# Chunked attention in transposed form on block-diagonal operands, placed between the matmuls of a feed-forward layer

## The chip, the cores and the metric

The kernel runs on one core of a Trainium2 chip. The metric is the time of one execution on the device in microseconds (us), the median over several runs. One execution of each kernel is also recorded by the hardware profiler; times inside a kernel are read from that record.

The engines: PE is TensorE (matmuls; PEld is its weight load), DVE is VectorE, ACT is ScalarE, POOL is GpSimd, SP is the sync engine, which here only issues DMAs.

## The reference

Attention inside chunks of 64 tokens, for 8 batches, 8 heads, 576 tokens and head dimension 64; its output, 4608 tokens of 512 numbers, goes through a feed-forward layer of width 2048 with exact gelu. The output is f32.

```python
scores = scale * np.matmul(q_c, k_c.transpose(0, 1, 2, 4, 3))      # 64 x 64 per chunk
scores = scores - np.max(scores, axis=-1, keepdims=True)
attn = np.exp(scores)
attn = attn / (np.sum(attn, axis=-1, keepdims=True) + 1e-09)
out = np.matmul(attn, v_c)
...                                     # heads side by side: x is (4608, 512)
h = x @ w_in                            # (512, 2048)
g = 0.5 * h * (1.0 + erf(h * inv_sqrt2))
return (g @ w_out).astype(np.float32)   # (2048, 512)
```

## The kernel before

Attention runs first, for all 64 pairs of batch and head; the feed-forward layer follows. Matmuls take bf16. Every small product goes to its own PSUM tile and is copied out by VectorE or ScalarE.

```python
    a_ps = ctx...tile_pool(name="a_ps", bufs=2, space=bass.MemoryType.PSUM)   # two buffers per tag
    ...
    for idx in range(B * H):
            for pi in range(NPAIR):              # transposes of q and k, 2 chunks at a time
                nc.tensor.transpose(tpq[0:CH*n_here, :], qb[:, c0:c0+n_here, :], identity_bf[:])
                nc.vector.tensor_copy(qT[0:CH*n_here, pi, :], tpq[0:CH*n_here, :])
                ...                              # the same for k, with nc.scalar.copy
            for c in range(NC):                  # NC = 9 chunks
                nc.tensor.matmul(sc_ps[:], qT[pp:pp+CH, pi, :], kT[pp:pp+CH, pi, :], tile_position=(pp, 0))
                ...                              # copy to sc_all, VectorE and ScalarE in turn
            nc.scalar.activation(ex[:], sc_all[:], mybir.ActivationFunctionType.Exp, scale=scale)
            ...                                  # row sums, reciprocal, product: attn_bf
            for c in range(NC):
                nc.tensor.transpose(atp[:], attn_bf[:, c, :], identity_bf[:])
                ...                              # copy to attn_T
            for c in range(NC):
                nc.tensor.matmul(o_ps[:], vb[:, c, :], attn_T[:, c, :])
                ...                              # copy to x_sbuf; odd heads by way of tmp and a DMA
    ...
    for mi in range(n_m_tiles):                  # 9 tiles of 512 tokens
        for nf in range(FF_sub):                 # 16
            for ks in range(K_sub):              # 4
                nc.tensor.matmul(h_ps[:], w_in_sbuf[:, ks, nf*P:(nf+1)*P],
                    x_sbuf[:, ks, mi*M_TILE:(mi+1)*M_TILE], start=(ks == 0), stop=(ks == K_sub - 1))
            nc.scalar.activation(h_sb[:, nf, :], h_ps[:], mybir.ActivationFunctionType.Gelu)
        for ms in range(n_m_subs):               # 4
            for nf in range(FF_sub):
                nc.tensor.matmul(y_ps[:], h_sb[:, nf, ms*P:(ms+1)*P], w_out_sbuf[:, nf, :],
                    start=(nf == 0), stop=(nf == FF_sub - 1))
            nc.vector.tensor_copy(y_sb[:], y_ps[:])
            nc.sync.dma_start(out_v[mi*M_TILE + ms*P : mi*M_TILE + (ms+1)*P, :], y_sb[:])
```

## Time and profile before

| | before |
|---|---|
| time, median | 665.89 us |
| span of the profiled execution | 664.4 us |
| attention, to the first feed-forward matmul | 410.1 us |
| feed-forward, its 1152 matmuls of 512 columns | 250.4 us |

The page of the kernel before. Part 1 gives busy time, share of the span and number of instructions of each engine; part 2 cuts the span into 40 slices and gives busy tenths in each.

```profile
span 664.4 us, 11364 instructions
...
PE 549.4 (83%) x3520; PEld 308.9 (46%) x3520; DVE 308.7 (46%) x1444; ACT 315.5 (47%) x1362; POOL 142.3 (21%) x200
...
PE   5468877777777777777777776999999999999997
...
DVE  4367777777777777677677773011010110101101
ACT  4346555565555555655555564432514325143250
```

PE is at 7 or 8 tenths up to slice 25 and at 9 from there on. That average hides two different stages. The table of stretches shows them apart (busy time and, in brackets, instructions that began, in 10 us of each stage):

```profile
core 0: us, PE busy (x) PEld busy (x) DVE busy (x) ACT busy (x) POOL busy (x), PEclk, DMA share, GB/s
300.00:310.00 10.00, 7.68 (x62) 5.03 (x61) 7.42 (x38) 5.55 (x32) 4.37 (x6) 1.00 0.70 48
450.00:460.00 10.00, 10.00 (x48) 4.53 (x47) 0.69 (x1) 2.89 (x5) 0.00 (x0) 1.00 0.07 26
```

In the second stretch PE is busy all the time with 217 ns a matmul (250.4 us / 1152), and everything else waits for it. (The clock of 1.00 in the first row can't be trusted: the trace's first record of the clock is at 413.4 us, and up to 413.0 us the feed-forward matmuls still start 0.427 us apart, half the later rate. The attention stage most likely ran at half clock.) In the first, no engine is full, and 62 small matmuls share 10 us. The chain of waits inside that stretch (start, length, what) says why:

```profile
301.70 0.27 PE atp L136 x2
301.99 0.21 ACT attn_T L138
302.21 0.04 issue
302.25 0.21 PE atp L136
302.50 0.21 ACT attn_T L138
```

Matmul, copy, matmul, copy: each link takes 0.2 us or a little more because the next matmul of the kind waits until one of two PSUM buffers has been copied out. Attention is bound by the latency of many small links, 6.4 us for each of 64 heads, and not by the throughput of an engine. This is read from the chain.

### The profile page before, as it was taken

The numbers are of one execution on the slowest core, as the hardware profiler recorded it, in microseconds if no ns is written. First come the engines' busy times: TensorE is split into PE (matmuls) and PEld (weight loads), VectorE is DVE, ScalarE is ACT, GpSimd is POOL, SyncE is SP. The second block draws the span as 40 slices with busy tenths as digits, with TensorE's granted clock in tenths as the row PEclk, the third lists the DMA queues.
The fourth block names the chain that finished last, engine by engine and source line by source line (L and its number), as shares of the span: only waits on it lengthen the run. The fifth ranks groups of instructions, "written<-read, shape, count | busy, mean of one in ns | idle before, by whom it ended". The sixth has DMA issues, their size and how long they took to land.

```text
span 664.4 us, 11364 instructions
## 1 busy us (share of the span) xinstructions
PE 549.4 (83%) x3520; PEld 308.9 (46%) x3520; DVE 308.7 (46%) x1444; ACT 315.5 (47%) x1362; POOL 142.3 (21%) x200
## 2 busy tenths in 40 slices
PE   5468877777777777777777776999999999999997
PEld 3244545454544554545454543444444444444443
DVE  4367777777777777677677773011010110101101
ACT  4346555565555555655555564432514325143250
POOL 9153333333332343333333100000000000000000
PEclk9999999999999999999999999999999999999999
DMA  9996566466656665665666200010010100101001
GB/s 86 207 117 46 42 46 46 34 48 47 44 40 45 43 47 40 47 47 39 43 48 42 20 8 8 16 48 32 33 65 16 48 32 33 64 16 48 35 30 63
DMA packets 144541, 30.90 MB, mean 47 GB/s; under 512 B 137312, under 2 KB 139360, under 8 KB 144480
## 3 DMA queue, kind: packets, MB, share of 16 engines
q0 software_dynamic: 116256, 18.36, 37.2%
q1 hardware_dynamic: 28224, 11.82, 6.5%
q8 instruction: 27, 0.44, 0.3%
q14 instruction: 34, 0.28, 0.1%
HBM read 36.70 MB, written 9.44 MB: 69 GB/s over the span
## 4 chain that ended last, share of the span: by engine, by line
PE 69%; ACT 12%; DMA 7%; DVE 6%; issue 5%; POOL 0%; ACTq 0%; DVEq 0%; POOLq 0%
PE h_ps L174 19%; PE y_ps L187 19%; PE atp L136 10%; DMA x_sbuf<-tmp 7%; PE o_ps L144 7%; ACT attn_T L138 6%; PE tpq L103 5%; PE tpk L106 5%; PE sc_ps L114 4%; DVE attn_bf L131 3%; ACT kT L107 3%; ACT x_sbuf L150 2%; DVE x_sbuf L148 2%; ACT ex L125 1%; ACT sc_all L122 0%
## 5 line engine op out<-in xcount | busy, mean ns | idle before, releaser
L181 ACT ACTIVATE h_sb<-h_ps 128x512 bf16<-128x512 f32 x144 | 85.9, 597 | 148.1 <-PE h_ps L174 148.1
L144 PE MATMUL o_ps<-attn_T,vb 64*64 64x64 bf16 x576 | 115.6, 231 | 31.4 <-ACT tmp L156 11.7
L136 PE MATMUL atp<-identity_bf,attn_bf 64*64 64x64 bf16 x576 | 100.4, 230 | 38.1 <-ACT attn_T L138 15.4
L195 DVE COPY y_sb<-y_ps 128x512 f32<-128x512 f32 x36 | 24.9, 692 | 226.3 <-PE y_ps L187 226.3
L174 PE MATMUL h_ps<-x_sbuf,w_in_sbuf 128*128 128x512 bf16 x576 | 127.4, 383 | 1.1 <-DVE tmp L154 1.1
L187 PE MATMUL y_ps<-w_out_sbuf,h_sb 128*128 128x512 bf16 x576 | 125.8, 379 | 0.0
L138 ACT COPY attn_T<-atp 64x64 bf16<-64x64 bf16 x320 | 65.3, 204 | 93.9 <-PE atp L136 71.7
L114 PE MATMUL sc_ps<-kT,qT 64*64 64x64 bf16 x576 | 100.3, 239 | 4.7 <-ACT sc_all L122 3.3
L103 PE MATMUL tpq<-identity_bf,qb 64*128 64x64 bf16 (+1 forms) x320 | 69.7, 218 | 30.5 <-ACT kT L107 22.4
L144 PEld LDWEIGHTS <-vb 64*64 64x64 bf16 x576 | 68.9, 135 | 45.0 <-issue 36.0
L174 PEld LDWEIGHTS <-w_in_sbuf 128*128 128x128 bf16 x576 | 56.6, 98 | 70.9 <-issue 2.2
L187 PEld LDWEIGHTS <-h_sb 128*128 128x128 bf16 x576 | 56.4, 98 | 67.9
L136 PEld LDWEIGHTS <-attn_bf 64*64 64x64 bf16 x576 | 63.4, 137 | 52.0 <-DVE attn_bf L131 28.0
L107 ACT COPY kT<-tpk 128x64 bf16<-128x64 bf16 (+1 forms) x320 | 66.3, 207 | 43.1 <-PE tpk L106 31.4
L72 POOL DMA_DIRECT2D kb<-in_k_dram x64 | 47.4, 740 | 173.5 <-PE tpk L106 99.8
L120 DVE COPY sc_all<-sc_ps 64x64 f32<-64x64 f32 x320 | 65.5, 211 | 24.0 <-PE sc_ps L114 21.3
L106 PE MATMUL tpk<-identity_bf,kb 64*128 64x64 bf16 (+1 forms) x320 | 71.6, 224 | 5.3 <-DMA kb<-in_k_dram 0.8
L114 PEld LDWEIGHTS <-qT 64*64 64x64 bf16 x576 | 54.4, 130 | 38.0 <-issue 30.9
L104 DVE COPY qT<-tpq 128x64 bf16<-128x64 bf16 (+1 forms) x320 | 55.2, 173 | 19.8 <-PE tpk L106 8.4
L71 POOL DMA_DIRECT2D qb<-in_q_dram x64 | 47.7, 746 | 44.4 <-PE o_ps L144 23.9
L140 DVE COPY attn_T<-atp 64x64 bf16<-64x64 bf16 x256 | 45.8, 179 | 23.8 <-PE atp L136 10.9
L122 ACT COPY sc_all<-sc_ps 64x64 f32<-64x64 f32 x256 | 52.7, 206 | 6.7 <-PE sc_ps L114 5.6
(21 smaller groups left out, 394.4 us busy)
## 6 DMA issues: line engine op xcount, KB each, us to landing
out_dram<-y_sb SPq DMA_DIRECT2D x36, 256.0 KB, 2.0
qb<-in_q_dram POOLq DMA_DIRECT2D x64, 72.0 KB, 2.8
kb<-in_k_dram POOLq DMA_DIRECT2D x64, 72.0 KB, 2.7
vb<-in_v_dram POOLq DMA_DIRECT2D x64, 72.0 KB, 2.8
x_sbuf<-tmp SPq DMA_DIRECT2D x288, 8.0 KB, 1.9
w_in_sbuf<-in_moe_w_in_dram POOLq DMA_DIRECT2D x1, 2048.0 KB, 14.4
w_out_sbuf<-in_moe_w_out_dram POOLq DMA_DIRECT2D x1, 2048.0 KB, 24.4
```

What stands on the lines that cost most here:

```text
L103: nc.tensor.transpose(tpq[0:CH*n_here, :], qb[:, c0:c0+n_here, :], identity_bf[:])
L104: nc.vector.tensor_copy(qT[0:CH*n_here, pi, :], tpq[0:CH*n_here, :])
L106: nc.tensor.transpose(tpk[0:CH*n_here, :], kb[:, c0:c0+n_here, :], identity_bf[:])
L107: nc.scalar.copy(kT[0:CH*n_here, pi, :], tpk[0:CH*n_here, :])
L114: nc.tensor.matmul(sc_ps[:], qT[pp:pp+CH, pi, :], kT[pp:pp+CH, pi, :], tile_position=(pp, 0),)
L120: nc.vector.tensor_copy(sc_all[:, c, :], sc_ps[:])
L136: nc.tensor.transpose(atp[:], attn_bf[:, c, :], identity_bf[:])
L138: nc.scalar.copy(attn_T[:, c, :], atp[:])
L144: nc.tensor.matmul(o_ps[:], vb[:, c, :], attn_T[:, c, :])
L174: nc.tensor.matmul(h_ps[:], w_in_sbuf[:, ks, nf*P:(nf+1)*P], x_sbuf[:, ks, mi*M_TILE:(mi+1)*M_TILE], start=(ks == 0), stop=(ks == K_sub - 1),)
L181: nc.scalar.activation(h_sb[:, nf, :], h_ps[:], mybir.ActivationFunctionType.Gelu)
L187: nc.tensor.matmul(y_ps[:], h_sb[:, nf, ms*P:(ms+1)*P], w_out_sbuf[:, nf, :], start=(nf == 0), stop=(nf == FF_sub - 1),)
```

## The change

The intent: cut the number of instructions of attention, and hide what is left of it behind the dense stream of the feed-forward layer.

- **Form.** Two heads are handled at once. Their keys, and their values, are laid out as blocks on the diagonal of 128x128 operands whose other blocks are zero. Scores come out transposed (keys on the partitions), so that exp of them can go straight into the value matmul: no transpose of the attention, no copy of the scores. Sums come from one matmul with a block-diagonal matrix of ones. The maximum is not subtracted, in either kernel.
- **Unit.** A unit is two heads times 512 tokens. There are 9 tiles of 512 tokens and 4 units in each. A unit has three parts: T (8 transposes, 3 copies on VectorE), S (8 score matmuls, an exp on ScalarE), B (the sum matmul, 8 value matmuls, 4 instructions on VectorE that divide and write x).
- **Placement.** The order is fixed by hand. T of tile t+1 stands between the first matmuls of tile t; S and B of tile t+1 stand between the second matmuls of tile t-1.
- **Loads.** q and k come in f32 as rows of 1 KB on the sync queue and are cast on GpSimd (tile 0: on VectorE and ScalarE). v comes by casting DMAs on the GpSimd queue into the zeroed diagonals.

The core of the diff, cut:

```diff
-    for idx in range(B * H):
-        ...
+    def att_T(t, g):
+        tp = ps_tp.tile([P, 2, J, P], bf16, tag="tp", name="tp")
+        for w, nm in enumerate(("q", "k")):
+            for j in range(J):                                          # J = 4
+                nc.tensor.transpose(tp[:, w, j, :], st[nm][:, g, j]..., ident[:])
+        nc.vector.tensor_copy(qT[:].rearrange("p i j c -> p j i c"), tp[:, 0]...)
+        for r in range(2):
+            sl = slice(CH * r, CH * (r + 1))
+            nc.vector.tensor_copy(
+                k_bd[sl, :, sl].rearrange("p i (c j) -> p j i c", j=J),
+                tp[sl, 1].rearrange("p j (i c) -> p j i c", i=CT))
+    def att_S(t, g):
+        for i in range(CT):                                             # 8 chunks
+            nc.tensor.matmul(s_ps[:, i, :], st["k_bd", g][:, i, :], st["qT", g][:, i], ...)
+        nc.scalar.activation(pT[:], s_ps[:], Act.Exp, scale=scale)
+    def att_B(t, g):
+        nc.tensor.matmul(sum_ps[:], ones_bd[:], pT[:], start=True, stop=True)
+        for i in range(CT):
+            nc.tensor.matmul(av_ps[:, i, :], st["v"][:, i, g, :], pT[:, i, :], ...)
+        nc.vector.transpose(t1[:], sum_ps[:]...)
+        nc.vector.reciprocal(r1[:], t1[:, :, 0])
+        nc.vector.transpose(rc[:], r1[:].to_broadcast([P, NB, 32]))
+        nc.vector.tensor_tensor(
+            x[:, g, :].rearrange("p (i c j) -> p i j c", i=CT, j=J),
+            av_ps[:]..., rc[:]..., op=mybir.AluOpType.mult)
+    with tc.manual_schedule():
+        new_tile(0)                     # loads of q, k, v of tile 0
+        ...                             # 4 DMAs of w_in
+        new_tile(1)
+        ...                             # 2 DMAs of w_out
+        new_tile(2)
+        T, S_, Bs = att_units(0)
+        for u in T + S_ + Bs:
+            u()
+        T, S_, Bs = att_units(1)        # issues the casts of tile 1 on GpSimd
+        run_phase(mm1_slot, 0, FF, {4: [T[0]], 5: [T[1]], 6: [T[2]], 7: [T[3]],
+                                    9: [S_[0]], 10: [S_[1]], 11: [S_[2], Bs[0]], 12: [S_[3]],
+                                    13: [Bs[1]], 14: [Bs[2]], 15: [Bs[3]]})
+        for t in range(1, NT):
+            ...                         # att_units(t + 1), new_tile(t + 2)
+            run_phase(mm1_slot, t, FF, {1: [T[0]], 5: [T[1]], 9: [T[2]], 13: [T[3]]} if nxt else {})
+            run_phase(mm2_slot, t - 1, 16,
+                      {1: [S_[0]], 3: [S_[1]], 5: [S_[2], Bs[0]], 7: [S_[3], Bs[1]],
+                       9: [Bs[2]], 11: [Bs[3]]} if nxt else {})
+        run_phase(mm2_slot, NT - 1, 16, {})
```

A slot is 4 matmuls of 512 columns, 0.86 us; a phase is 16 slots.

## The prediction

> **What bounds the kernel now.** Two stages follow one another. In the timeline the first feed-forward matmul (line 174) starts at 410.09 us and the last of line 187 ends at about 660.5; one VectorE copy (0.69 us) and a store end the span of 664.4 us. In the second stage PE is saturated: the table of stretches has it busy 240.0 of 240 us, and 1152 matmuls in 250.4 us are 217 ns each. The Trainium skill ("TensorE: Matmul & The Clock Gate", Back-to-back issue gap) gives N/2.4 + 2.5 ns, 216 at N=512; the trace agrees.
>
> The first 410 us are attention, 6.4 us a head, with no engine saturated. The chain of waits alternates matmul (0.21 us) and eviction (0.20 us) through two PSUM buffers per tile kind; costs are per instruction, over a thousand small ones each on PE, ACT and DVE.
>
> **What the change does.** (1) A unit is two heads by 512 tokens, 36 in all: 8 transposes, 8 score matmuls, one 512-wide sum matmul, 8 value matmuls. The transposes of the attention, the score copies and the 288 stores into x's upper half go. (2) Units of tile t+1 stand between matmuls of tiles t and t-1, so their DVE and ACT work hides under the 217 ns stream. (3) q and k come as 1 KB f32 rows on the sync queue and are cast on GpSimd; v comes by casting DMA into zeroed block diagonals.
>
> **Costs (estimates from the trace's durations).** DVE per unit: three evictions of 0.6 us, two 512-wide block transposes, a reciprocal (0.20), a product (0.74): 4.2 us, 150 in all, plus 25 for y: hidden. ACT: gelu 86 us, 36 exps of 0.6, some 25 table loads of 1.28: hidden except in the first phase. GpSimd per tile: 16 DMA issues of up to 0.74 and 8 casts of 0.8, against 35 us: hidden. PE per unit: 24 small matmuls at 0.08 to 0.10 us (a 128-column weight load lasts 98 ns) plus 0.22: 2.3 us, wholly on the critical path.
>
> **Sum.**
> - Prologue: 43 us. 18 zeroing memsets on DVE stand before the first casts (20 us), then casts, 4 units of evictions (7) and 4 chains of 2.6, with nothing to hide under.
> - First phase, tile 0: 13.8 + 4 x 2.3 + 10 of stalls (exps among gelus switch tables about 8 times, and tile 1's x is wanted at once): 33 us.
> - Sixteen phases of 13.8: 221; 28 units x 2.3: 64; stalls 5: 290 us.
> - Last 16 slots 13.8, copy and store 4: 18 us.
>
> Total **384 us**, range 358 to 425. Chances: faster by over 2% 0.98, within 2% 0.01, slower 0.01.
>
> **What would show it right or wrong.** PE is dense after 43 us; feed-forward matmuls stay 216 ns apart. The wait table has PE's main waits in the prologue and around tile 0's phase, little elsewhere. The chain of waits is over 80% PE. The prologue is wrong if the first h matmul starts before 34 or after 52 us; the unit cost is wrong if a tile's two phases take other than 27.6 + 9 us.
>
> **What would make it wrong.** GpSimd too slow (46 DMA issues stand ahead of tile 1's casts; or casts over 2 us); strided evictions much slower than 0.6 us; the last unit's product arriving late for the next phase, every tile; small matmuls over 0.12 us; start-up loads (over 12 MB asked for at once) holding back tile 0's q and k or the first weights.

## The result, and the profile after

The changed kernel takes 375.31 us (median of 4 runs, 374.62 to 376.38), against 665.66 us in the same rounds: a ratio of 0.5635, with a 95% interval of 0.562 to 0.565.

The page after, the lines that answer to those of before, with GpSimd and the granted clock added:

```profile
span 374.2 us, 5238 instructions
...
PE 305.2 (82%) x2052; PEld 154.5 (41%) x2052; DVE 239.6 (64%) x313; ACT 140.2 (37%) x208; POOL 125.2 (33%) x204
...
PE   0353500766899999999999999999999999999995
...
DVE  7989100696775975887598589759867965920221
ACT  2130200189564066236505622551563165254000
POOL 7321855989700007703920780270130000000000
PEclk9999955598999999999999999999999999999999
```

PE is dense from slice 12 on. But there is a hole in slices 6 and 7, from 43.7 us on, and the granted clock falls to one half there (slices 6 to 8). PE's waits (who waited for whom, total, times, longest):

```profile
PE tp L148 <- POOL q_nat L115: 22.6, 1, 22.6
PE tp L148 <- DVE q_nat L111: 12.8, 1, 12.8
PE av_ps L180 <- DVE x L190: 5.8, 7, 0.8
...
PE h_ps L212 <- DVE x L190: 4.3, 3, 2.4
```

One wait of 22.6 us for the casts of tile 1 on GpSimd is larger than all others. Once past the start, a tile looks like this in the timeline of PE (start, length, instruction, idle before it):

```profile
130.10 0.39 PE L148 MATMUL tp<-ident,q_nat 128*128 128x128 bf16 x4
130.33 0.39 PE L148 MATMUL tp<-ident,k_nat 128*128 128x128 bf16 x4
130.55 3.63 PE L212 MATMUL h_ps<-x,w_in_sb 128*128 128x512 bf16 x16
...
145.71 0.40 PE L167 MATMUL s_ps<-qT,k_bd 128*128 128x64 bf16 x8
145.95 1.89 PE L224 MATMUL y_ps<-w_out_sb,h 128*128 128x512 bf16 x8
...
149.87 0.38 PE L177 MATMUL sum_ps<-pT,ones_bd 128*128 128x512 bf16 x1
150.08 0.40 PE L180 MATMUL av_ps<-pT,v_bd 128*128 128x64 bf16 x8
150.32 1.89 PE L224 MATMUL y_ps<-w_out_sb,h 128*128 128x512 bf16 x8
...
153.48 0.41 PE L180 MATMUL av_ps<-pT,v_bd 128*128 128x64 bf16 x8 [0.82 <-DVE x L190]
```

The length of such a row includes the latency of the last matmul; the cost to the stream is the distance between starts. Eight transposes cost 130.55 - 130.10 = 0.45 us, eight score matmuls 0.24, the sum 0.21 and eight value matmuls 0.24: 1.14 us a unit. The only idle time on PE in the tile is 0.82 us, in the last line shown: the value matmuls of the second unit want a PSUM buffer that VectorE's product for the first unit still reads.

The sum of the prediction against the trace (the first matmul of tile 1 is worked out as 94.07 + 4 x 0.216 = 94.9 us, the start of the last 16 slots as 342.37 + 64 x 0.216 = 356.2 us, from rows that merge several phases):

| stretch | predicted | measured |
|---|---|---|
| prologue, to the unbroken feed-forward stream | 43 | 38.8 |
| first phase, tile 0, with the units of tile 1 | 33 | 56.1 |
| 16 phases with 28 units | 290 | 261.3 |
| last 16 slots, copy and store | 18 | 18.0 |
| sum | 384 | 374.2 |

The total was near, and two of its terms were off by some 25 us each, in opposite directions. The experiments ask about both, and about where the gain comes from.

**Theories.** (A) The hole comes from the order of GpSimd's instructions: the casts stand behind 46 DMA issues, some of which wait for the weights to land. Rival: the start is bound by DMA bandwidth, and the casts only show it. (B) A small matmul with its own weight load costs 0.03 us of the stream, and this is on the critical path. Rivals: 0.08 to 0.10 us, as predicted; or PE has slack. (C) The placement is worth as much as the form. Rival: the form alone does it. (D) VectorE's writes with a step are what makes its part long. (E) Table loads stall the first phase, as predicted; rival: they hide.

### The profile page after: what moved, and what is told of

It reads as the page before. It is cut to its first block, busy times and chain, and to the rows that moved or that the text cites. A ratio compares the mean times of both kernels' runs of the same rounds, so it can differ in the third digit from the quotient of the medians.

```text
span 374.2 us, 5238 instructions
## 1 busy us (share of the span) xinstructions
PE 305.2 (82%) x2052; PEld 154.5 (41%) x2052; DVE 239.6 (64%) x313; ACT 140.2 (37%) x208; POOL 125.2 (33%) x204
## 4 chain that ended last, share of the span: by engine, by line
PE 65%; DVE 14%; DMA 13%; POOL 4%; issue 2%; DVEq 0%; POOLq 0%
PE h_ps L212 30%; PE y_ps L224 28%; DMA w_in_sb<-in_moe_w_in_dram 7%; DVE x L190 4%; DMA w_out_sb<-in_moe_w_out_dram 4%; PE tp L148 4%; POOL v_bd L124 3%; DMA v_bd<-in_v_dram 3%; DVE rc L188 3%; DVE k_bd L157 3%; DVE t L184 3%; PE s_ps L167 1%; PE av_ps L180 1%; PE sum_ps L177 1%; DVE r L186 1%
## 5 line engine op out<-in xcount | busy, mean ns | idle before, releaser
L212 PE MATMUL h_ps<-x,w_in_sb 128*128 128x512 bf16 x576 | 138.1, 390 | 4.4 <-DVE x L190 4.3
L214 ACT ACTIVATE h<-h_ps 128x512 bf16<-128x512 f32 x144 | 85.5, 597 | 144.7 <-PE h_ps L212 144.5
L224 PE MATMUL y_ps<-w_out_sb,h 128*128 128x512 bf16 x576 | 132.5, 379 | 0.0
L124 POOL DMA_DIRECT2D v_bd<-in_v_dram x128 | 83.9, 713 | 29.4 <-DMA w_in_sb<-in_moe_w_in_dram 12.8
L157 DVE COPY k_bd<-tp 64x512 bf16<-64x512 bf16 x72 | 92.6, 1287 | 0.5
L212 PEld LDWEIGHTS <-w_in_sb 128*128 128x128 bf16 x576 | 55.7, 100 | 65.4 <-issue 9.3
L224 PEld LDWEIGHTS <-h 128*128 128x128 bf16 x576 | 53.5, 98 | 58.1
L115 POOL CAST q_nat<-q_f 128x512 bf16<-128x512 f32 x32 | 18.4, 637 | 106.8 <-PE h_ps L212 58.6
L190 DVE TENSOR_TENSOR x<-av_ps,rc 128x512 bf16<-128x512 f32 x36 | 46.5, 1292 | 4.1 <-DVE rc L188 0.5
L148 PE MATMUL tp<-ident,q_nat 128*128 128x128 bf16 x144 | 15.5, 236 | 39.7 <-POOL q_nat L115 22.6
L184 DVE STREAM_TRANSPOSE t<-sum_ps 128x512 f32<-128x512 f32 x36 | 25.7, 715 | 8.8 <-PE sum_ps L177 8.8
L188 DVE STREAM_TRANSPOSE rc<-r 128x512 f32<-128x512 f32 x36 | 25.6, 711 | 1.3
L115 POOL CAST k_nat<-k_f 128x512 bf16<-128x512 f32 x32 | 18.4, 628 | 8.5 <-DMA k_f<-in_k_dram 7.8
## 6 DMA issues: line engine op xcount, KB each, us to landing
k_f<-in_k_dram SPq DMA_DIRECT2D x2, 896.0 KB, 11.5
```

Source lines behind the costliest of these rows:

```text
L115: nc.gpsimd.tensor_copy(o[:, g], i_[:, g])
L124: nc.gpsimd.dma_start(v_bd[CH * r:CH * (r + 1), i0:i0 + n, g, CH * r:CH * (r + 1)], v[b, 2 * g + r, CH * cs:CH * (cs + n), :].rearrange("( ...
L148: nc.tensor.transpose(tp[:, w, j, :], st[nm][:, g, j].rearrange("p r d -> p (r d)"), ident[:])
L157: nc.vector.tensor_copy(k_bd[sl, :, sl].rearrange("p i (c j) -> p j i c", j=J), tp[sl, 1].rearrange("p j (i c) -> p j i c", i=CT))
L184: nc.vector.transpose(t1[:], sum_ps[:].rearrange("p (n e) -> p n e", e=32))
L188: nc.vector.transpose(rc[:], r1[:].to_broadcast([P, NB, 32]))
```

## The experiments

Twelve variants were run besides the changed kernel; all gave correct results.

| kernel | time, us | ratio to before |
|---|---|---|
| the changed kernel | 375.3 | 0.5635 |
| e1_cast_first | 359.6 | 0.5401 |
| e2_serial | 519.8 | 0.7806 |
| e3_slot8 | 381.0 | 0.5722 |
| e4_double | 381.7 | 0.5737 |
| e5_swap | 372.7 | 0.5600 |
| e6_group | 362.3 | 0.5438 |
| e7_three | 339.4 | 0.5098 |
| e8_four | 341.9 | 0.5127 |
| e9_best | 343.4 | 0.5153 |
| e10_wout_last | 366.5 | 0.5506 |
| e11_ungroup | 340.5 | 0.5115 |
| e12_prologue | 335.4 | 0.5038 |

### e2_serial: the form without the placement

```diff
+        for t in range(NT):
+            T, S_, Bs = att_units(t)
+            ...
+            for u in T + S_ + Bs:
+                u()
-        run_phase(mm1_slot, 0, FF, {4: [T[0]], 5: [T[1]], ...})
+        run_phase(mm1_slot, 0, FF, {})
         for t in range(1, NT):
-            run_phase(mm1_slot, t, FF, {1: [T[0]], ...} if nxt else {})
-            run_phase(mm2_slot, t - 1, 16, {1: [S_[0]], ...} if nxt else {})
+            run_phase(mm1_slot, t, FF, {})
+            run_phase(mm2_slot, t - 1, 16, {})
```

> All units of all nine tiles run before the first feed-forward matmul (x kept for nine tiles; some rotating buffers cut from 3 to 2 to make room); the transposed block-diagonal form is as in the changed kernel. Theory (the placement hides some 6 us of VectorE work per unit): attention becomes bound by VectorE at 6.0 us per unit, 36 x 6.0 = 215 us plus the start and the 23 us hole, and the feed-forward follows at 250 us: 490-520 us. Rival (the form alone does it, VectorE and PE of neighbouring units overlap by themselves and the placement adds little): under 430 us.

Measured: 519.8 us. The form alone takes 666.2 - 519.8 = 146 us off, the placement another 519.8 - 375.3 = 145 us: (C) holds, in this order: the parts of the form (pairs of heads on the diagonal, transposed scores, fewer and larger copies, other loads) were not run apart, nor was the placement without the form. Busy time in 100 us of the attention stage and in the feed-forward stage:

```profile
core 0: us, PE busy (x) PEld busy (x) DVE busy (x) ACT busy (x) POOL busy (x), PEclk, DMA share, GB/s
...
100.00:200.00 100.00, 40.18 (x407) 29.89 (x408) 92.09 (x115) 9.12 (x16) 63.73 (x103) 0.60 0.78 111
262.00:512.00 250.00, 250.00 (x1154) 112.94 (x1153) 29.49 (x43) 85.97 (x144) 0.00 (x0) 0.99 0.10 37
```

VectorE is busy 92 of 100 us there and PE 40. That is the work that the placement hides: while VectorE needs about 6 us a unit, the feed-forward stream runs beside it.

### e4_double: what does a small matmul cost?

```diff
-        for i in range(CT):
+        for i in list(range(CT)) * 2:
             nc.tensor.matmul(s_ps[:, i, :], st["k_bd", g][:, i, :], st["qT", g][:, i],
```

> Every score matmul is issued twice, the second writing the same values to the same place: 288 more matmuls of 64 columns, each with its weight load. Theory (PE's stream is the critical path and a small matmul with its own load costs what the trace's spacing shows, 0.029 us): 0.235 us per unit on 32 units in or near the stream: +7 to +9 us. By the prediction's 0.08 to 0.10 us each: +23 to +29 us. Rival (PE has slack in the steady part): +2 us or less.

Measured: 381.7 us, 6.4 us more, a little less than the 7 to 9 expected. In the steady state a tile takes 33.87 us (128.63 to 162.50) where the changed kernel takes 33.16 (129.24 to 162.40). The four units' added matmuls explain 4 x 0.24 = 0.94 us of that; 0.22 us came back, since the wait of 0.82 us at the second unit shrank to 0.60. So (B) holds: these matmuls are on the critical path, at 0.029 us each with their own weight load. The predicted 0.08 to 0.10 us would have given 23 us or more. The Trainium skill ("TensorE: Matmul & The Clock Gate", "Wait — 56ns, not 53.3ns?") gives about 25 ns as the least distance between two matmuls, however short; the 29 ns at 64 columns and 56 ns at 128 (0.45 us / 8) lie above that, and no run here tests the floor itself. What fits them is the formula N/2.4 + 2.5 that my prediction quoted for 512 columns only: it gives 29 and 56 ns. I should have used it instead of the 98 ns that a weight load lasts. The load lasts that long but overlaps its neighbours.

### e1_cast_first and e10_wout_last: the hole

```diff
         new_tile(1)
+        tiles[1]["cast"]()              # e1_cast_first: before w_out and the v loads of tile 2
         for c in range(2):
             ...                         # w_out
         new_tile(2)
         ...                             # att_units no longer issues the casts of tile 1
```

> The q and k casts of tile 1 on GpSimd are issued before the two DMAs of w_out and the v loads of tile 2; nothing else changes. Theory (GpSimd's order): PE's 22.6 us wait for q_nat comes from the 18 DMA issues that stand ahead of the casts and that wait in turn for w_in and w_out to land; q and k of tile 1 had landed long before. Then the wait falls to about 3 us, the cold matmuls after it go too, and the time falls by about 20 us, to 353-357. Rival (the start-up is bound by DMA bandwidth, the casts merely reveal it): the wait moves to w_out, v of tile 1 or other loads and the time falls by under 8 us, to 367 or more.

Measured: 359.6 us, 15.7 us less. What GpSimd did before the casts in the changed kernel, in its timeline:

```profile
27.75 0.56 POOL L124 DMA_DIRECT2D v_bd<-in_v_dram  x1 [3.22 <-DMA w_in_sb<-in_moe_w_in_dram]
31.97 0.75 POOL L124 DMA_DIRECT2D v_bd<-in_v_dram  x1 [3.66 <-DMA w_in_sb<-in_moe_w_in_dram]
36.25 0.55 POOL L124 DMA_DIRECT2D v_bd<-in_v_dram  x1 [3.52 <-DMA w_in_sb<-in_moe_w_in_dram]
39.23 6.02 POOL L124 DMA_DIRECT2D v_bd<-in_v_dram  x9 [2.43 <-DMA w_in_sb<-in_moe_w_in_dram]
45.16 1.87 POOL L247 DMA_DIRECT2D w_out_sb<-in_moe_w_out_dram  x2
46.91 3.96 POOL L124 DMA_DIRECT2D v_bd<-in_v_dram  x6
54.45 0.60 POOL L124 DMA_DIRECT2D v_bd<-in_v_dram  x1 [3.58 <-DMA w_out_sb<-in_moe_w_out_dram]
59.87 5.76 POOL L124 DMA_DIRECT2D v_bd<-in_v_dram  x9 [4.82 <-DMA w_out_sb<-in_moe_w_out_dram]
65.52 2.39 POOL L115 CAST q_nat<-q_f 128x512 bf16<-128x512 f32 x4
```

It issued the v loads of tile 1, w_out and the v loads of tile 2, four times waiting for a w_in DMA and twice for a w_out DMA to land, and reached the casts at 65.52 us. PE's transposes of tile 1 began at 66.31. With the casts earlier, PE's waits for them are:

```profile
PE tp L148 <- POOL q_nat L115: 4.3, 2, 3.4
...
PE tp L148 <- POOL k_nat L115: 3.4, 2, 1.8
```

The largest wait for a cast is 3.4 us instead of 22.6. (A) holds. The gain is 4 us less than expected, because the same thing now happens on a small scale to tile 2, whose casts still stand behind w_out: PE waits 0.97 and 1.81 us for them at 77 us, and the 16 matmuls after that take 5.30 instead of 3.62 us, since the clock had dropped.

Why did GpSimd wait for w_out to land at all? Count the DMAs on its queue (numbers 1 to 16 come before the lines above): 8 of v (tile 0), 4 of w_in, 16 of v (tile 1), 2 of w_out, 16 of v (tile 2). In the lines above, numbers 17 to 20 wait for w_in, which is numbers 9 to 12, and numbers 37 and 38 wait for w_out, numbers 29 and 30. Each waits for the one eight places before it. (The program's instruction list had the same as waits for semaphores.)

So in this program at most eight DMAs of that queue are under way, and a large one blocks what stands eight places behind it, casts included. The second experiment parts this from the plain time to issue:

```diff
-        for c in range(2):              # w_out, ahead of new_tile(2)
-            ...
         T, S_, Bs = att_units(1)        # the casts of tile 1
+        for c in range(2):              # e10_wout_last
+            ...
```

> The changed kernel with only the two DMAs of w_out moved behind tile 1's casts on GpSimd; the 16 v loads of tile 2 stay ahead of them. This parts the 22.6 us hole into the landing of w_out, which GpSimd waits for since each of its DMAs waits for the one eight before it (12 us with their own issue), and the plain issue of 16 loads (10.4 us). If so, PE's wait for q_nat falls to 10-14 us and the time to 363-367. If the issue time alone makes the hole: wait of 20 us or more. If the landing alone: under 5 us.

Measured: 366.5 us, and a longest wait of 13.4 us for the cast:

```profile
PE tp L148 <- POOL q_nat L115: 13.4, 1, 13.4
```

So some 9 us of the hole were w_out's issue and landing, 10 us the issue of the 16 v loads of tile 2, and the rest lay before that. In these runs bandwidth is part of the cause only through the waits for landing.

### e3_slot8: the wait of 0.82 us

```diff
-                      {... 5: [S_[2], Bs[0]], 7: [S_[3], Bs[1]], 9: [Bs[2]], 11: [Bs[3]]}
+                      {... 5: [S_[2], Bs[0]], 7: [S_[3]], 8: [Bs[1]], 10: [Bs[2]], 12: [Bs[3]]}
```

> The value units B1, B2 and B3 stand one slot later in the second feed-forward phase (slots 8, 10, 12 in place of 7, 9, 11); nothing else changes. Theory: PE waits 0.82 us in each of 7 tiles because B1's value matmuls want the PSUM buffer that B0's product on VectorE has not released; one slot of 0.86 us covers it. The waits for that product vanish in the steady tiles and the time falls by 5 to 6 us (1.5%). Rival: the wait only moves to the next unit or to the next tile's x (VectorE's chain of 2.95 us a unit sets the pace): change under 2 us.

Measured: 381.0 us, 5.7 us *more*. My theory fell. The wait at the second unit did vanish, but a larger one came:

```profile
PE tp L148 <- POOL q_nat L115: 24.8, 1, 24.8
PE h_ps L212 <- DVE x L190: 13.5, 10, 2.4
```

Ten waits of the feed-forward matmuls for x, 13.5 us in all, in place of three of 4.3. With the last unit one slot later, its product on VectorE ends after the next tile's first matmuls want x: about 1.3 us of waiting in each tile, against 0.82 saved. A tile went from 33.16 to 33.75 us (130.30 to 164.05). VectorE's chain of about 2.95 us a unit fixes when the last x is ready, and the placement had no room to give. The hole was also 2.2 us longer in this run (24.8 us).

### e5_swap: VectorE's strided writes

The same elements in another order: neighbours in the output come one after the other, and PSUM is read with a step.

```diff
-                k_bd[sl, :, sl].rearrange("p i (c j) -> p j i c", j=J),
-                tp[sl, 1].rearrange("p j (i c) -> p j i c", i=CT))
+                k_bd[sl, :, sl].rearrange("p i (c j) -> p i c j", j=J),
+                tp[sl, 1].rearrange("p j (i c) -> p i c j", i=CT))
 ...
-            x[:, g, :].rearrange("p (i c j) -> p i j c", i=CT, j=J),        # and av_ps, rc alike
+            x[:, g, :].rearrange("p (i c j) -> p i c j", i=CT, j=J),
```

> The changed kernel with only the order turned round in which VectorE walks the same elements in two instructions: the two k_bd evictions and the product into x now write neighbouring elements one after the other and read PSUM with a stride, in place of reading in runs and writing every fourth element. Theory (the write with a step of four 2-byte elements is what makes them 1.29 us): k_bd falls to 0.7 us or less, the product to 0.75-0.85 us, VectorE per unit from 6.0 to about 4.3 us; the 0.82 us waits in 7 tiles vanish (5.7 us), the prologue shortens by 4 x 1.7 = 6 to 7 us and the stretch of tile 1's units by some us; the hole at the casts grows by what the prologue wins, since GpSimd sets its end. Sum: 6 to 11 us less, 364-369. Rival (half of the partitions, or the PSUM read, is what is slow): durations stay within 10% or grow, and so does the time.

The groups of VectorE, first of the changed kernel, then of e5_swap (out<-in, shapes, count, busy us and mean ns of one, idle before):

```profile
L157 DVE COPY k_bd<-tp 64x512 bf16<-64x512 bf16 x72 | 92.6, 1287 | 0.5
L190 DVE TENSOR_TENSOR x<-av_ps,rc 128x512 bf16<-128x512 f32 x36 | 46.5, 1292 | 4.1 <-DVE rc L188 0.5
...
L150 DVE COPY qT<-tp 128x512 bf16<-128x512 bf16 x36 | 15.2, 423 | 51.6 <-PE tp L148 51.4
```

```profile
L157 DVE COPY k_bd<-tp 64x512 bf16<-64x512 bf16 x72 | 49.2, 684 | 0.5
L190 DVE TENSOR_TENSOR x<-av_ps,rc 128x512 bf16<-128x512 f32 x36 | 36.4, 1010 | 4.1 <-DVE rc L188 0.5
...
L150 DVE COPY qT<-tp 128x512 bf16<-128x512 bf16 x36 | 15.3, 424 | 89.0 <-PE tp L148 88.9
```

The k_bd copies went from 1287 to 684 ns and the product from 1292 to 1010 ns; the qT copy, which was not touched, stayed. So the order in which elements are walked was the cost, and not the half of the partitions: (D) holds for k_bd, and the product fell less than expected. The swap changed the read along with the write. But the qT copy reads PSUM in the same order as the k_bd copy of the changed kernel, writes runs of 16 neighbours and takes 423 ns, so the step of 4 in the write is what is left for the 1287. The Trainium skill ("SBUF — State Buffer", on cachelines of 16 bytes) says that steps of up to 8 bf16 elements run at full rate; here a step of 4 elements on the write side took nearly twice as long as the other order, so the measurement decides.

The time, 372.7 us, fell by 2.6 us only, less than the 6 to 11 expected. The wait of 0.82 us in each tile shrank to about 0.54 and did not vanish. And the prologue did get shorter, with the stream beginning at 33.25 us instead of 38.79, but PE then waited 29.9 us for the casts instead of 22.6. The hole swallowed the gain, and tile 1's transposes, which GpSimd's casts release, began at 67.99 us, later than the 66.31 of the changed kernel. This is the clearest lesson on the way: while one engine's order sets the end of a stretch, speeding up another engine there only lengthens the wait.

### e6_group, e7_three, e8_four, e11_ungroup: tables, and the causes together

e6_group is e1_cast_first with tile 1's exps in a row, so that ScalarE switches tables twice in the first phase in place of eight times:

```diff
-                                    9: [S_[0]], 10: [S_[1]], 11: [S_[2], Bs[0]], 12: [S_[3]],
+                                    9: [S_[0], S_[1], S_[2], S_[3]], 11: [Bs[0]],
```

> As e1_cast_first, with tile 1's four score units together in slot 9 of the first feed-forward phase, so that its four exps follow one another on ScalarE: the table loads in that phase go from about 8 to 2. Prediction's step (the table switches stall that phase by about 10 us): 6 to 10 us less than e1_cast_first (359.6). Rival (there it is VectorE's chain, 3 us per unit, that PE waits for, and ScalarE's loads hide behind it): within 2 us of e1_cast_first.

Measured: 362.3 us, 2.7 us *slower* than e1_cast_first. The six spared table loads of 1.28 us won nothing, and the fourth score unit now waits 2.5 us for a PSUM buffer. Nor does any wait of PE's in the changed kernel name ScalarE. So the predicted stall from table switches is not there: (E) falls. A switch cost 1.31 us between the end of a gelu (78.10 us in the changed kernel) and the start of the exp (79.41). The Trainium skill ("ScalarE: Activation LUTs", "What ACT_TABLE_LOAD costs") adds a drain of about 1.38 us to the load of 1.28; the trace shows none.

e7_three joins the three, with the casts of tiles 1 and 2 ahead of their v loads:

```diff
-        new_tile(1)
+        tiles[1] = load_qk(1)
+        tiles[1]["cast"]()
+        tiles[1]["v"] = load_v(1)
+        tiles[2] = load_qk(2)
+        tiles[2]["cast"]()
         ...                             # w_out
-        new_tile(2)
+        tiles[2]["v"] = load_v(2)
```

> The casts of tiles 1 and 2 on GpSimd go ahead of the v loads of the same tile and of w_out, with the turned element order of e5_swap and the grouped exps of e6_group. If the causes are separate (GpSimd's order 16 to 20 us, VectorE's strided writes 10 us or more once the hole no longer swallows the prologue's gain): 338-348 us, PE's wait for q_nat under 2 us. If the start is bound by the loads, the wait moves to w_in or v and it stays above 350.

Measured: 339.4 us, 36 us below the changed kernel, and no wait for a cast on GpSimd is left among PE's waits. Cheaper VectorE work, worth 2.6 us by itself, should be part of that: the stream begins at 33.23 us, and no hole swallows it. How much is owed to it and how much to the earlier casts of tile 2 was not run apart.

> As e7_three, with the value units one slot later as in e3_slot8. Theory (e3_slot8 lost since VectorE's chain for the last unit then ended after the next tile's first matmuls wanted x; with a shorter chain it ends in time): within 1 us of e7_three either way, since the turned order already removes the wait that the shift was for. Rival (the shift itself costs something else): 4 to 6 us slower than e7_three.

e8_four, with the shift of e3_slot8 added, took 341.9 us: 2.5 us slower than e7_three, between the two expectations. PE's waits for x in front of feed-forward matmuls went from 5.0 us (3 times) to 11.2 us (11 times). The shift costs less with the shorter chain, but it still costs.

> As e7_three with the exps of tile 1 in the first feed-forward phase placed as in the changed kernel, so with about 8 table loads there in place of 2. Grouping cost e1_cast_first 2.7 us (e6_group); if that was since VectorE's chain hid the loads, then with VectorE's shorter chain the loads show and this is 1 to 4 us slower than e7_three (339.4). If the table loads never matter: 1 to 3 us faster than e7_three.

e11_ungroup, e7_three with the exps placed as in the changed kernel, took 340.5 us (ratio 0.5115, interval 0.5098 to 0.5132, against 0.5098, 0.5088 to 0.5107, for e7_three). The intervals overlap; PE does wait 2.4 us for gelus and 1.1 us for exps there, and it loses as much elsewhere with the grouping. Whether grouping helps with the cheaper VectorE work stays unclear at 1 us.

### e9_best and e12_prologue: the prologue

Both put only the zeroing that tile 0 needs ahead of its casts, and use one f32 buffer for q and k in place of two, so that later tiles' loads hold back.

```diff
-    for i, t_ in enumerate(v_bds):      # all 18 memsets ahead of the casts on VectorE
+    zero_v(v_bds[0])
+    for t_ in k_bds[:G]:
+        zero_k(t_)
 ...
+        cast1(0), T[0]()                # e9_best
+        zero_v(v_bds[1])
+        cast1(1), T[1](), S_[0]()
+        zero_v(v_bds[2])
+        cast1(2), T[2](), S_[1](), Bs[0]()
+        cast1(3), T[3](), S_[2](), Bs[1](), S_[3](), Bs[2](), Bs[3]()
```

> As e7_three without the grouped exps, and with a shorter prologue: only the zeroing that tile 0 needs stands ahead of its first cast on VectorE, tile 0's cast, transposes, scores and values follow one another by pair of heads, and q and k of tiles 1 and 2 have one f32 buffer in place of two, so that they are not loaded while tile 0 and w_in are. If the prologue (33 us to the first unbroken feed-forward stream in e7_three) is VectorE's order, it shrinks to 24-28 us and the time to 330-336 us. If the landing of w_in is what sets it by now, the first stream stalls on w_in and the time stays at 337-342.

e9_best took 343.4 us, 4 us more than e7_three: a miss, of which the exps left ungrouped can explain about 1 us (e11_ungroup). VectorE took its instructions in the order written, and in this order it waited about 1.1 us for PE after each of the four casts, and each later cast waited for the zeroing and for the copies before it. The unbroken stream began at 35.51 us, later than e7_three's 33.23.

```diff
+        for t_ in v_bds[1:]:            # e12_prologue: on GpSimd, behind the issue of w_in
+            zero_v(t_, nc.gpsimd)
+        ...
+        tiles[0]["cast1"](0)
+        for g in range(G):
+            if g + 1 < G:
+                tiles[0]["cast1"](g + 1)        # one pair ahead
+            T[g]()
+        for u in S_ + Bs:
+            u()
```

> As e7_three; on VectorE only the zeroing for tile 0 stays ahead of tile 0's casts, the rest goes to GpSimd behind the issue of w_in; tile 0's casts run one pair ahead of the transposes; one f32 buffer for q and k, so that later tiles' loads wait. e9_best lost since casts, zeroing and evictions took turns on VectorE. If VectorE's order sets the prologue, the first unbroken feed-forward stream starts at 27-30 us in place of 33.2 and the time is 333-337 us. If w_in's landing sets it, PE waits on w_in and the time is 338 or more.

Measured: 335.4 us, the fastest of all, with a ratio of 0.5038 to the kernel before. Its timeline of PE:

```profile
6.80 0.61 PE L151 MATMUL tp<-ident,q_nat 128*128 128x128 bf16 x4 [6.80 <-DVE q_nat L118]
...
28.11 5.19 PE L215 MATMUL h_ps<-x,w_in_sb 128*128 128x512 bf16 x13 [2.18 <-DVE x L193]
33.13 0.39 PE L151 MATMUL tp<-ident,q_nat 128*128 128x128 bf16 x4
```

The first transposes start at 6.80 us, the stream at 28.11, and the transposes of tile 1 follow at 33.13 without a wait. PE does not wait for w_in. e9_best had the single f32 buffer too and gained nothing, so it was VectorE's work that set the prologue. Its order and the zeroing moved to GpSimd were not run apart.

## Why the prediction was right or wrong

The total was right: 384 us predicted, 358 to 425 as the range, 375.3 measured. It was right by luck: two errors of some 25 us cancelled. By its own tests the prediction failed in three places. PE was not dense after 43 us, for the hole of 22.6 us came; a tile took 33.16 us and not 27.6 + 9; and the first h matmul started at 33.82 us, just before the 34 that it named as the limit.

- **What bounded the kernel before, and what the change hides: right.** The feed-forward stream keeps its 216 ns a matmul, and e2_serial shows that VectorE's work, about 6 us a unit, is what hides. The chain of waits is PE by 65% only, where I had said over 80%.
- **"PE per unit: 24 small matmuls at 0.08 to 0.10 us ... 2.3 us": the size was wrong.** It is 1.14 us. On 28 units that is 64 - 32 = 32 us too much. That PE's part is wholly on the critical path was right (e4_double). The step that failed was to take the length of a weight load as its cost.
- **"First phase, tile 0: ... 10 of stalls ... 33 us": wrong in size and cause.** It took 56.1 us. Of that, 18.4 us are matmuls (13.8 + 4 x 1.14), 24.2 us are waits for GpSimd's casts (22.58 + 1.60), 6.6 us other waits, mostly for VectorE, and most of the remaining 7 us must be matmuls at half rate, by their spacing (below). The table switches, named as a main part of the 10 us, had no share that grouping them could win back (e6_group). The wait for GpSimd stands in the prediction as a risk ("46 DMA issues stand ahead of tile 1's casts") but was left out of the sum: "GpSimd per tile ... hidden" counted its work per tile and not the queue that it starts with.
- **Prologue: 43 us predicted, 38.8 measured.** Two errors again: zeroing ran in 11.5 us instead of 20 (the six large memsets took 0.91 us each, as 32-bit words), and the copies into k_bd took 1.29 us instead of 0.6.
- **Steady tiles: right.** Little waiting there, 0.82 us a tile. It did lie on VectorE's chain of a unit, as the list of risks said of the last unit's product.

The hole also cost speed after it. Part 2 of the page after shows PEclk at 5 tenths in slices 6 to 8, and four feed-forward matmuls in a row took 1.91 us at 68.92 us and 1.03 us at 73.81 us. The Trainium skill ("TensorE: Matmul & The Clock Gate", "What's actually happening") says that an idle window of about 3.4 us halves the clock and a busy one restores it. For the hole and its end the trace agrees. But the clock was also at half from about 83.8 to 87.2 us (four matmuls took 1.90 us at 84.59), although none of PE's waits since 73.5 us was longer than 1.34 us. In the 3.41 us before this drop PE was still busy for 1.39 us. So the trace shows that a window need not be wholly idle.

## What to carry to other kernels

Hiding one stage behind another's dense matmul stream was worth as much here as making that stage cheaper: 145 and 146 us. After it, the start decides: look at every in-order queue, the DMA-issuing engine first of all, and ask what stands ahead of the first instruction that the dense stream needs. Cost small matmuls by the distance between starts, and judge a speed-up of one engine only when no other engine sets the end of the same stretch.

## What the Trainium skill lacked or had wrong

- "TensorE: Matmul & The Clock Gate", "Back-to-back issue gap": it gives about 81 ns a matmul at 128 columns for a stream in which each has its own weight load. Here 128-column transposes with a load each came every 56 ns, and 64-column matmuls with a load each every 29 ns. For 512 columns the same sentence gives about 131 ns, and here it is 217. The formula N/2.4 + 2.5, which the page calls that of an isolated matmul, fits all three (56, 29 and 216 ns).
- "TensorE: Matmul & The Clock Gate", "Part 4: PE-mode transpose": about 275 ns for a 128x128 transpose in a kernel. That is near the length of one in the record (236 ns); between two in a row it is 56 ns.
- "ScalarE: Activation LUTs", "What ACT_TABLE_LOAD costs": 2.66 us a switch with a drain. Here 1.31 us from the end of one function to the start of the other, 1.28 of it the load.
- "SBUF — State Buffer", on cachelines: steps of up to 8 bf16 elements at full rate. A copy of 64x512 bf16 from PSUM that writes with a step of 4 elements took 1287 ns, and 684 ns with neighbours written in turn and PSUM read with a step. "VectorE: DVE Perf Modes" has one element a cycle as its slowest mode, whatever the step: at its 0.96 GHz an estimate of 533 ns for 512 elements, to which the start of the instruction comes. The 684 ns are near that; the 1287 are more than twice it.
- "TensorE: Matmul & The Clock Gate", "Seeing it yourself", warns that recorded clock events can be unreliable and tells of a clock stuck for over 50 us. It does not say what to make of the time before the first event. Here that is at 42.8 us, and the page of the profile shows PEclk 9 in slices 1 to 5, while feed-forward matmuls from 39.2 to 42.6 us (slice 5) started 0.427 us apart in place of 0.216.
